# Batch 0's shuffle split between SBUF-to-SBUF moves and DRAM, and later shuffles sent in two parts, in a fused DFT and gated-MLP kernel

## The chip, the cores and the metric

The kernel runs on one core of a Trainium2 chip. The metric is the device time of one execution in microseconds (us). Before the change nine runs gave a median of 633.46 us (630.8 to 638.19). One further execution was profiled; all durations of single instructions come from it.

The engines are TensorE (PE; its weight loads are shown apart as PEld), VectorE (DVE), ScalarE (ACT), GpSimd (POOL) and SyncE (SP, which here only issues transfers). Every engine works through its own queue in order. Transfers are issued by SP, ACT and POOL and carried out by the core's 16 DMA engines.

## The reference, cut to what matters

```python
x = 0.1 * randn(8, 3008, 256)                      # batch, sequence, width; f32
X = fft(fft(x, axis=1), axis=2).real               # along the sequence, then along the width
X = X.reshape(24064, 256)
out = (relu(X @ w_gate) * (X @ w_val)) @ w_out     # 256 -> 1536 -> 256, f32
```

## The kernel before, in words

**Sequence DFT in two stages.** 3008 = 94 x 32. A batch lies in SBUF with 94 partitions and 32 rows j of 256 numbers in each. Since x is real, row j and row 32 - j are folded into one another (`fold`, on POOL, for batches 1 to 7), which leaves 17 rows in the tile `eo`. Stage 1 (`stage1`, line 152) multiplies each of 16 rows j by a table `w1[:, j, :]` of 96 columns: 48 frequencies, cosine and sine. The result goes through PSUM into the tile `t1` (96 partitions, 16 rows j). Stage 2 contracts over j and over cosine and sine, so these must become partitions: `t4` has 128 partitions (4 groups of frequencies x cosine or sine x 16 rows j) and 12 blocks of 256 numbers. The way from t1 to t4 is the **shuffle**: `shuffle_out` (line 202) writes t1 to a DRAM buffer `Td`, and `shuffle_in` (line 207) reads it back in the other order, in pieces of 512 bytes. `rotate` (line 213) then mends one column of t4 by a small matmul with the matrix `rot` and a copy back, and `stage2` (line 221) multiplies by the table `m2` and leaves `pq`, the operand of the MLP. Its second half (cs = 1) also sends one row to DRAM and back as a broadcast, `nb`.

**The width DFT** is folded into the weights: `pair_w` adds and subtracts the halves of a weight, `fold_w` (line 281) multiplies by cosines and sines of the width, and `wc`, `ws` and `wm` are the weights that the MLP uses.

**Start.** Batch 0 isn't folded. Its rows come by six loads on POOL's queue (`load_first`, line 119) that cast f32 to bf16: rows 0 to 15 into the tile `lo` by plain loads, rows 16 to 31 in mirrored order into `hi` by indirect loads. Each partition gets four or eight rows as one contiguous piece. `first_products` (line 180) then does stage 1 with separate matmuls for both tiles, in the groups of pairs c = (1, 2, 3), (4, 5) and (6, 7, 0), where pair c holds the rows 2c and 2c + 1; `evacuate` (line 167) copies each pair from PSUM to t1 on ACT or DVE. Batch 0's t1 leaves in four transfers (pairs 1 to 3, 4 and 5, 6 and 7 on SP; pair 0 on ACT), and comes back in two on SP (blocks 0 to 3, then 4 to 11), ahead of the loads of the other weights. `warm` (line 348) issues matmuls on a tile of zeros (`wk`, into `psk`): 11 at the start, 10 after the products, 7 more (line 490) ahead of the first rotate. Only blocks 0 to 3 are rotated before the main loop; the others at its step 4 (line 683).

**Main loop.** 288 steps of 8 batches x 3 blocks x 12 slices of the MLP's inner width. A step t does the gate's and the value's matmuls for one slice (lines 557, 558, 564 and 572), and the output matmuls of the block before (line 621). Work on the next batch is put between the steps by hand: `at(t, ...)` lists what is issued at a step, `plan` gives the steps of the eight stage 1 pairs of the next batch, `sh`, `tr` and `t2` those of its shuffle, rotate and stage 2. `pace` hands the steps of `fold` to POOL at a fixed rate. A later batch's shuffle leaves in one transfer (768 KB) after the eighth pair and comes back in one.

Of the kernel before, what the change touches and what calls it, by code (L numbers as in the profile page):

```python
# [43 lines left out]
def kernel(ctx: ExitStack, tc, x, w_gate, w_val, w_out, out):  # L44
# [32 lines left out]
    JH, PAD = NB // 4, 4  # L77
# [18 lines left out]
    def fold(b, eng):  # L96


        eo = xt[b]["eo"] = tp.tile([96, J, D], BF16, tag="eo", name="eo")[0:NA]
        for half, chunks in enumerate(((1, 3, 5, 7), (9, 11, 13))):  # L100
            for lo in chunks:
                xl, xh = xt[b][half]
                n, o = (3 if lo == 13 else 2), lo - half * (JH + 1)
                x1, e1, m = xl[0:NA, o:o + n, :], eo[:, lo:lo + n, :], (NB // 2 - lo - (0 if half else JH)) * D
                eng.tensor_tensor(free(e1, 0, [D, n], [H, 2]), free(x1, 0, [D + PAD, n], [H, 2]),
                                  free(xh[0:NA], m, [-D, n], [H, 2]), op=ALU.add)
                yield eng.tensor_tensor(x1[:, :, 1:D], x1[:, :, 1:D],  # L107
                                        free(xh[0:NA], m + D - 1, [-D, n], [-1, D - 1]), op=ALU.add)
                for op, o in ((ALU.add, 1), (ALU.subtract, H + 1)):
                    yield eng.tensor_tensor(e1[:, :, o:o + H - 1], x1[:, :, 1:H],  # L110
                                            free(x1, D - 1, [D + PAD, n], [-1, H - 1]), op=op)
            src, j = xt[b][half][0][0:NA, JH - 1 if half else 0, :], J - 1 if half else 0
            eng.tensor_copy(free(eo[:], j * D, [H, 2]), free(src, 0, [H, 2]))
# [5 lines left out]
    def load_first(r, n):  # L119

        name = "lo" if r < NB // 2 else "hi"
        if name not in xt.setdefault(0, {}):
            xt[0][name] = tp.tile([96, J, D], BF16, tag="eo", name=name)
        dst = xt[0][name][:, r % 16:r % 16 + n, :]
        if r < NB // 2:
            nc.gpsimd.dma_start(out=dst, in_=view(x, r * D, [[NB * D, 96], [1, n * D]]))
        else:
            k = {(24, 8): 0, (20, 4): 1, (16, 4): 2}[r, n]
            nc.gpsimd.indirect_dma_start(
                out=dst.rearrange("p j d -> p (j d)"), out_offset=None,  # L130
                in_=view(x, 0, [[n * D, NB // n * NA], [1, n * D]]),
# [20 lines left out]
    def stage1(b, c, evac):  # L152

        ps, eo = borrow("ps1"), xt[b]["eo"]
        for i in range(2):
            jj = 2 * c + i
            o = ps[0:96, i * D:(i + 1) * D]
            if jj:
                nc.tensor.matmul(o, lhsT=w1[:, jj, :], rhs=eo[:, jj, :], start=True, stop=True)  # L159
                continue  # L160
# [19 lines left out]
    def first_products(c, upper):  # L180
# [3 lines left out]
        for i in range(2):  # L184
            jj = 2 * c + i
            o = psf[c][0:96, i * D:(i + 1) * D]
            v = xt[0]["hi"][0:NA, 0 if jj == 0 else NB // 2 - jj, :] if upper else xt[0]["lo"][0:NA, jj, :]
# [19 lines left out]
    def shuffle_in(b, a0, a1):  # L207
        if b not in t4t:
            t4t[b] = tp.tile([128, NKA, D], BF16, tag="t4", name="t4")
        nc.sync.dma_start(out=t4t[b][:, a0:a1, :],  # L210
                          in_=view(Td[b], a0 * 128 * D, [[D, 128], [128 * D, a1 - a0], [1, D]]))

    def rotate(b, a0=0, a1=NKA, evac=nc.scalar.copy):
        t4 = t4t[b]
        ps = borrow("psr") if b or a0 else early("psr")
        nc.tensor.matmul(ps[:, a0:a1], lhsT=rot[:], rhs=t4[:, a0:a1, H], start=True, stop=True)
        evac(t4[:, a0:a1, H], ps[:, a0:a1])
# [85 lines left out]
    with tc.tile_pool(name="sp", bufs=1, space=SB) as sp:  # L303
# [24 lines left out]
        ki = sp.tile([NA, NKA, 4], F32, tag="ki")  # L328
# [8 lines left out]
        di = sp.tile([128, 4, 2, 16], F32, tag="di")  # L337
        ro = sp.tile([128, 4, 2, 16], F32, tag="ro")
# [17 lines left out]
        iota(pl, ki[:], [[1, NKA], [NKA, 4]], 0, 0)  # L356
# [18 lines left out]
        iota(pl, di[:], [[-32, 4], [-16, 2], [-1, 16]], 0, 1)  # L375
# [10 lines left out]
        def table(a, b_):  # L386
            cosines(free(w1[:], 96 * a, [96, b_ - a], [2, 48]), tq[:, a:b_, :], S)
            sines(free(w1[:], 96 * a + 1, [96, b_ - a], [2, 48]), tt[:, a:b_, :], S, -1.0)
# [28 lines left out]
        jj, sl, up = bits(0, 15), bits(4, 1), bits(5, 3)  # L417
# [5 lines left out]
        both = (free(tt[:], 0, [16 * 48, 2], [1, 48]), free(tq[:], 0, [16 * 48, 2], [1, 48]))  # L423
        cosines(free(wz[:], 0, [97, 2], [2, 48]), both[1], S)
        for k in range(2):
            sines(free(wz[:], 192 * (k + 1), [97, 2], [2, 48]), both[0], S, 2.0 * k - 1.0)
# [33 lines left out]
        evacuate(0, 7, psf[7], "dve")  # L460
        evacuate(0, 0, psf[0], "act")
        shuffle_out(0, 6, 8)
        shuffle_out(0, 0, 1, nc.scalar)
# [4 lines left out]
        shuffle_in(0, 0, 4)  # L468
        shuffle_in(0, 4, NKA)
# [3 lines left out]
        pl.tensor_scalar(ro[:, :, 0, 1:16], di[:, :, 0, 1:16], scalar1=16.0, scalar2=-1.0,  # L473
                         op0=ALU.is_equal, op1=ALU.mult)
        pl.tensor_scalar(ro[:, :, 1, 1:16], di[:, :, 1, 1:16], scalar1=-16.0, scalar2=None, op0=ALU.is_equal)
        pl.tensor_scalar(ro[:, :, :, 0], di[:, :, :, 0], scalar1=0.0, scalar2=None, op0=ALU.is_equal)
        pl.tensor_copy(rot[:], ro[:].rearrange("p u s j -> p (u s j)"))
        pl.iota(ix[:], pattern=[[-1, 2], [4 * NA, B]], base=4 * NA - 1, channel_multiplier=-4)
        pl.tensor_scalar(ix[:], ix[:], scalar1=0, scalar2=None, op0=ALU.max)

# [8 lines left out]
        psk = psg.tile([128, 512], F32, tag="g", name="psk")  # L489
        warm(7)  # L490
        rotate(0, 0, 4, dve.tensor_copy)
# [15 lines left out]
        for k in range(3, 12):  # L507
# [175 lines left out]
    at(4, rotate, 0, 4, NKA)  # L683
# [9 lines left out]
    for b in range(B - 1):  # L693
# [4 lines left out]
        at(t0 + sh, shuffle_out, b + 1, 0, 8)  # L698
        at(t0 + sh, shuffle_in, b + 1, 0, NKA)
        at(t0 + tr, rotate, b + 1)  # L700
        for i, k in enumerate(t2):
            at(t0 + k, stage2, b + 1, i // 2, i % 2, "act")
# [7 lines left out]
    def pace(t):  # L710

        paced["due"] += 0 if t < 12 else 1 if t < 23 else 0.75 if t < 54 else 23 / 36
# [83 lines left out]
```

## Time and profile before

| | |
|---|---|
| median of nine runs | 633.46 us (630.8 to 638.19) |
| profiled execution, its own time | 636.28 us |
| span of the profiled execution, first to last instruction | 634.1 us |
| TensorE busy | 620.2 us, 98% |
| VectorE busy | 536.1 us, 85% |
| ScalarE busy | 438.9 us, 69% |
| GpSimd busy | 517.7 us, 82% |
| DMA | 69.03 MB, mean 109 GB/s |
| mean granted TensorE clock | 0.989 |

In the lines of the profile, L592 is line 592 of the kernel before, `a<-b` says that a was written from b, and xN counts instructions. A line of waits names the engine, line and tile that waited, what released it, and then the total in us, how often, and the longest. A piece of the chain has its start and its duration in us. The granted clock is a share of TensorE's full speed; a table by stage gives it for each stretch of time.

### The profile page before, as it was taken

The numbers are of one execution on the slowest core, as the hardware profiler recorded it, in microseconds if no ns is written. First come the engines' busy times: TensorE is split into PE (matmuls) and PEld (weight loads), VectorE is DVE, ScalarE is ACT, GpSimd is POOL, SyncE is SP. The second block draws the span as 40 slices with busy tenths as digits, with TensorE's granted clock in tenths as the row PEclk, the third lists the DMA queues.
The fourth block names the chain that finished last, engine by engine and source line by source line (L and its number), as shares of the span: only waits on it lengthen the run. The fifth ranks groups of instructions, "written<-read, shape, count | busy, mean of one in ns | idle before, by whom it ended". The sixth has DMA issues, their size and how long they took to land.

```text
span 634.1 us, 12016 instructions
## 1 busy us (share of the span) xinstructions
PE 620.2 (98%) x4322; PEld 415.8 (66%) x4322; DVE 536.1 (85%) x641; ACT 438.9 (69%) x842; POOL 517.7 (82%) x443
## 2 busy tenths in 40 slices
PE   8999998999999999999999999999999999999996
PEld 6524665666667666666666666666666666666665
DVE  5567886899988988898988989889988999899991
ACT  4357776777777777777687777776777777766661
POOL 7089898999988999888988999889888966555665
PEclk7799999999999999999999999999999999999999
DMA  8579427442726146531836137342643123312114
GB/s 184 191 160 171 101 83 190 113 109 76 206 69 143 39 131 168 126 93 36 226 85 149 34 91 206 93 107 62 188 89 79 34 82 100 73 36 63 36 34 98
DMA packets 44050, 69.03 MB, mean 109 GB/s; under 512 B 5969, under 2 KB 33498, under 8 KB 41974
## 3 DMA queue, kind: packets, MB, share of 16 engines
q1 hardware_dynamic: 39062, 52.08, 32.5%
q0 software_dynamic: 4656, 15.88, 10.6%
q8 instruction: 34, 0.56, 0.4%
q10 hardware_dynamic: 272, 0.30, 0.2%
q14 instruction: 26, 0.21, 0.1%
HBM read 39.63 MB, written 30.96 MB: 111 GB/s over the span
## 4 chain that ended last, share of the span: by engine, by line
PE 95%; DMA 2%; DVE 1%; issue 0%; POOL 0%; ACT 0%; POOLq 0%; ACTq 0%; DVEq 0%
PE po L621 39%; PE V L572 19%; PE G L564 10%; PE G L557 9%; PE G L558 9%; PE psw L285 2%; PE ps L159 2%; PE ps L197 2%; PE ps L228 2%; DMA hi<-in_x_dram,ixf 1%; DMA t<-Td 1%; PE psk L351 1%; DMA Td<-t 1%; DVE h L585 0%; PE ps L163 0%
## 5 line engine op out<-in xcount | busy, mean ns | idle before, releaser
L592 POOL TENSOR_TENSOR h<-gm,E 128x992 bf16<-128x992 f32 (+1 forms) x138 | 319.8, 2318 | 80.1 <-DVE E L599 48.1
L621 PE MATMUL po<-wo,h 128*128 128x256 bf16 (+2 forms) x2304 | 328.6, 272 | 0.0
L621 PEld LDWEIGHTS <-h 128*128 128x128 bf16 (+2 forms) x2304 | 231.3, 103 | 105.9
L566 ACT ACTIVATE gm<-G 128x496 f32<-128x496 f32 (+1 forms) x288 | 170.5, 592 | 93.9 <-PE G L564 86.3
L585 DVE TENSOR_TENSOR h<-gs,V 128x1024 bf16<-128x1024 f32 (+3 forms) x150 | 173.8, 1159 | 62.8 <-PE V L572 47.8
L579 DVE SCALAR_TENSOR_TENSOR E<-nb,af,V 128x496 f32<-128x496 bf16 (+1 forms) x276 | 190.2, 731 | 0.0
L559 ACT ACTIVATE gs<-G 128x497 f32<-128x497 f32 (+2 forms) x288 | 169.6, 589 | 25.0 <-PE G L558 25.0
L599 DVE SCALAR_TENSOR_TENSOR E<-E,V 128x992 f32<-128x992 f32 (+1 forms) x138 | 164.4, 1192 | 0.0
L564 PE MATMUL G<-pq,wm 128*128 128x496 bf16 (+1 forms) x288 | 108.0, 375 | 0.3 <-ACT gs L559 0.2
L557 PE MATMUL G<-pq,wc 128*128 128x497 bf16 (+2 forms) x288 | 107.9, 375 | 0.0
L558 PE MATMUL G<-pq,ws 128*128 128x497 bf16 (+2 forms) x288 | 107.9, 375 | 0.0
L572 PE MATMUL V<-pq,ws 128*128 128x497 bf16 (+2 forms) x288 | 85.4, 374 | 0.0
L572 PE MATMUL V<-pq,wc 128*128 128x497 bf16 (+2 forms) x288 | 85.4, 375 | 0.0
L558 PEld LDWEIGHTS <-ws 128*128 128x128 bf16 x288 | 28.2, 98 | 32.6
L634 ACT COPY os<-po 128x512 f32<-128x512 f32 x63 | 36.9, 586 | 14.4 <-PE po L621 13.5
L174 ACT CAST t<-ps 96x512 bf16<-96x512 f32 x60 | 35.0, 583 | 12.4 <-PE ps L197 10.0
L572 PEld LDWEIGHTS <-wc 128*128 128x128 bf16 x288 | 28.2, 98 | 21.1 <-issue 3.0
L110 POOL TENSOR_TENSOR eo<-xla 94x254 bf16<-94x254 f32 x56 | 40.3, 727 | 0.7
L557 PEld LDWEIGHTS <-wc 128*128 128x128 bf16 x288 | 28.2, 98 | 18.5 <-issue 1.3
L107 POOL TENSOR_TENSOR xla<-xla,xha 94x510 f32<-94x510 f32 x28 | 35.5, 1267 | 2.2
L110 POOL TENSOR_TENSOR eo<-xlb 94x254 bf16<-94x254 f32 (+1 forms) x42 | 34.1, 815 | 0.6
L564 PEld LDWEIGHTS <-wm 128*128 128x128 bf16 x288 | 28.1, 98 | 7.5 <-issue 4.9
(119 smaller groups left out, 377.2 us busy)
## 6 DMA issues: line engine op xcount, KB each, us to landing
out_dram<-os SPq DMA_DIRECT2D x124, 128.0 KB
Td<-t SPq DMA_DIRECT2D x7, 768.0 KB
t<-Td SPq DMA_DIRECT2D x7, 768.0 KB
out_dram<-os SPq DMA_DIRECT2D x82, 64.0 KB
xla<-in_x_dram SPq DMA_DIRECT2D x7, 720.0 KB
xlb<-in_x_dram SPq DMA_DIRECT2D x6, 640.0 KB
nb<-Nd SPq DMA_DIRECT2D x23, 128.0 KB
out_dram<-os SPq DMA_DIRECT2D x40, 48.0 KB
```

What stands on the lines that cost most here:

```text
L110: yield eng.tensor_tensor(e1[:, :, o:o + H - 1], x1[:, :, 1:H], free(x1, D - 1, [D + PAD, n], [-1, H - 1]), op=op)
L557: nc.tensor.matmul(G[:, ds], lhsT=wc[0][:, fs], rhs=pq[:, 0, ds], start=True, stop=False)
L558: nc.tensor.matmul(G[:, ds], lhsT=ws[0][:, fs], rhs=pq[:, 1, ds], start=False, stop=True)
L559: nc.scalar.activation(pair(t, "gs")[:, t % 2, ds], G[:, ds], ACTF.Relu)
L564: nc.tensor.matmul(G[:, cols], lhsT=wm[0][:, f * 128:(f + 1) * 128], rhs=pqt[b, blk][:, 1, cols], start=False, stop=True, skip_group_check ...
L566: nc.scalar.activation(pair(t, "gm")[:, t % 2, cols], G[:, cols], ACTF.Relu)
L572: nc.tensor.matmul(pair(t, "V")[:, t % 2, cs], lhsT=w[:, f * 128:(f + 1) * 128], rhs=pqt[b, blk][:, min(k, 1), cs], start=(k == 0), stop=( ...
L579: nc.vector.scalar_tensor_tensor(pair(t, "E")[:, t % 2, cols], nbt[b, blk][:, cols], af[:, f:f + 1], pair(t, "V")[:, t % 2, cols], op0=ALU ...
L585: nc.vector.tensor_tensor(pair(t, "h")[:, k, 0, 0:ds.stop - ds.start], pair(t, "gs")[:, k, ds], pair(t, "V")[:, k, ds], op=ALU.mult)
L592: eng.tensor_tensor(free(pair(t, "h")[:], 1024 * (t % 2) + 512 + w - 1, [1024, n], [-1, w]), pair(t, "gm")[:, k, cols], val[:, k, cols], o ...
L599: nc.vector.scalar_tensor_tensor(E[:, :, cols], E[:, :, cols], 2.0, V[:, :, cols], op0=ALU.mult, op1=ALU.subtract)
L621: nc.tensor.matmul(po[0:m, i, :], lhsT=pair(t - f + ff, "h")[:, ff % 2, sg, g * 128:g * 128 + m], rhs=wo[:, ff, :], start=(ff == 0), stop= ...
```

## The change

- Batch 0's rows j = 0, 1 and 12 to 15 no longer pass through DRAM: for each, one transfer (`spread`) goes from t1 (96 partitions x 512 bytes) to t4 (8 partitions x 12 blocks). Three are issued by SP, three by ACT. Rows 2 to 11 go through Td as before, in two writes by SP, and come back by one read that POOL issues.
- For this the order of t4's partitions changes from (group, cosine or sine, j) to (j, group, cosine or sine). The columns of w1 and wz, the matrix rot and the index bits behind m2 change with it.
- Batch 0's t4 is rotated once, all 12 blocks, before the main loop. The seven `warm` matmuls ahead of it are gone, and so is the rotate at step 4.
- Later shuffles leave in three transfers: pairs 1 to 5 one step after the fifth pair's stage 1, then pairs 6 and 7, then pair 0. The read waits for all three and is in the new order.
- The loads of batch 0's rows ask for rows of 256 numbers (512 bytes in bf16): `lo` has rows at a distance of 258 numbers, and the source of `hi` is given row by row. The tile of `eo` has the same padded rows.
- stage2 does cs = 1 ahead of cs = 0 in the main loop, for batches 1 to 7. One step of batch 1's fold moves from before the main loop into it.

```diff
-    JH, PAD = NB // 4, 4
+    JH, PAD, DP = NB // 4, 4, D + 2
...
-        eo = xt[b]["eo"] = tp.tile([96, J, D], BF16, tag="eo", name="eo")[0:NA]
+        eo = xt[b]["eo"] = tp.tile([96, J, DP], BF16, tag="eo", name="eo")[0:NA]
...
-            xt[0][name] = tp.tile([96, J, D], BF16, tag="eo", name=name)
-        dst = xt[0][name][:, r % 16:r % 16 + n, :]
+            xt[0][name] = tp.tile([96, J, DP], BF16, tag="eo", name=name)
+        dst = xt[0][name][:, r:r + n, 0:D] if r < NB // 2 else free(xt[0][name][:], r % 16 * D, [1, n * D])
         if r < NB // 2:
-            nc.gpsimd.dma_start(out=dst, in_=view(x, r * D, [[NB * D, 96], [1, n * D]]))
+            nc.gpsimd.dma_start(out=dst, in_=view(x, r * D, [[NB * D, 96], [D, n], [1, D]]))
         else:
...
-                out=dst.rearrange("p j d -> p (j d)"), out_offset=None,
-                in_=view(x, 0, [[n * D, NB // n * NA], [1, n * D]]),
+                out=dst, out_offset=None,
+                in_=view(x, 0, [[n * D, NB // n * NA], [D, n], [1, D]]),
...
-    def shuffle_in(b, a0, a1):
+    def t4_of(b):
         if b not in t4t:
             t4t[b] = tp.tile([128, NKA, D], BF16, tag="t4", name="t4")
-        nc.sync.dma_start(out=t4t[b][:, a0:a1, :],
-                          in_=view(Td[b], a0 * 128 * D, [[D, 128], [128 * D, a1 - a0], [1, D]]))
+        return t4t[b]
+
+    def shuffle_in(b, j0, j1, q=nc.sync):
+        q.dma_start(out=t4_of(b)[8 * j0:8 * j1, :, :],
+                          in_=view(Td[b], j0 * D, [[D, j1 - j0], [16 * NKA * D, 8], [16 * D, NKA], [1, D]]))
+
+    def spread(jj, q):
+        q.dma_start(out=t4_of(0)[8 * jj:8 * jj + 8, :, :], in_=t1t[0][:, jj, :])
...
         evacuate(0, 6, psf[6], "act")
         evacuate(0, 7, psf[7], "dve")
+        spread(12, nc.scalar)
         evacuate(0, 0, psf[0], "act")
-        shuffle_out(0, 6, 8)
-        shuffle_out(0, 0, 1, nc.scalar)
+        spread(13, nc.sync)
+        spread(14, nc.sync)
+        spread(15, nc.sync)
+        spread(0, nc.scalar)
+        spread(1, nc.scalar)
...
-        shuffle_in(0, 0, 4)
-        shuffle_in(0, 4, NKA)
         load_w(1, nc.sync)
         load_w(2, nc.sync)
...
         pl.tensor_scalar(ix[:], ix[:], scalar1=0, scalar2=None, op0=ALU.max)
+        shuffle_in(0, 2, 12, pl)
...
-        psk = psg.tile([128, 512], F32, tag="g", name="psk")
-        warm(7)
-        rotate(0, 0, 4, dve.tensor_copy)
+        rotate(0, dve.tensor_copy)
         stage2(0, 0, 0, "act")
...
-        for k in range(3, 12):
+        for k in range(3, 11):
             next(first)
...
-    at(4, rotate, 0, 4, NKA)
...
-        at(t0 + sh, shuffle_out, b + 1, 0, 8)
-        at(t0 + sh, shuffle_in, b + 1, 0, NKA)
+        at(t0 + plan[min(b, 1)][4] + 1, shuffle_out, b + 1, 1, 6)
+        at(t0 + sh, shuffle_out, b + 1, 6, 8)
+        at(t0 + sh, shuffle_out, b + 1, 0, 1)
+        at(t0 + sh, shuffle_in, b + 1, 0, 16)
         at(t0 + tr, rotate, b + 1)
         for i, k in enumerate(t2):
-            at(t0 + k, stage2, b + 1, i // 2, i % 2, "act")
+            at(t0 + k, stage2, b + 1, i // 2, 1 - i % 2, "act")
...
-        paced["due"] += 0 if t < 12 else 1 if t < 23 else 0.75 if t < 54 else 23 / 36
+        paced["due"] += 0 if t < 12 else 1 if t < 24 else 0.75 if t < 54 else 23 / 36
```

## The prediction

> **What bounds the kernel now.** I read the page first, then who waited for whom on TensorE, then a table by stage, then the chain in two stretches, then the transfers.
>
> The page (engine, busy us, share of the span, instructions):
>
> ```profile
> span 634.1 us, 12016 instructions
> PE 620.2 (98%) x4322; PEld 415.8 (66%) x4322; DVE 536.1 (85%) x641; ACT 438.9 (69%) x842; POOL 517.7 (82%) x443
> PE 95%; DMA 2%; DVE 1%; issue 0%; POOL 0%; ACT 0%; POOLq 0%; ACTq 0%; DVEq 0%
> ```
>
> TensorE is busy for 98% and carries 95% of the chain. Only two things shorten the run: fewer matmuls, or one of its few waits gone. These are the waits (total us, times, longest):
>
> ```profile
> PE psr L216 <- DMA t<-Td: 2.6, 1, 2.6
> PE V L572 <- DVE h L585: 1.5, 2, 1.0
> PE ps L197 <- DMA hi<-in_x_dram,ixf: 1.4, 1, 1.4
> PE psk L351 <- DVE wk L345: 1.3, 1, 1.3
> PE psw L285 <- ACT t L217: 0.5, 1, 0.5
> PE ps L197 <- DMA lo<-in_x_dram: 0.3, 1, 0.3
> ```
>
> The change touches the first, the third, the fifth and the sixth. The table by stage (us; busy of PE, PEld, DVE, ACT, POOL; granted clock; DMA share; GB/s):
>
> ```profile
> 0.00:9.00 9.00, 6.08 (x35) 3.02 (x36) 5.88 (x21) 5.46 (x11) 7.12 (x21) 0.99 0.72 113
> 9.00:20.50 11.50, 11.36 (x105) 11.24 (x105) 5.27 (x17) 2.77 (x8) 4.52 (x15) 0.50 0.65 184
> 20.50:24.00 3.50, 3.50 (x12) 1.25 (x12) 3.40 (x9) 1.25 (x3) 0.00 (x0) 0.71 0.29 84
> 24.00:29.50 5.50, 5.44 (x32) 1.94 (x28) 1.99 (x5) 1.75 (x3) 0.00 (x0) 1.00 0.94 299
> ```
>
> The products of batch 0 (line 197) run 9.14 to 20.44 at clock 0.50, although TensorE is never idle there. POOL is idle from 20.5 to 29.5. The chain around batch 0's shuffle and around batch 1's (start us, us, what):
>
> ```profile
> 20.44 3.24 PE psk L351 x10
> 23.68 2.73 PE psw L285 x12
> 26.41 1.62 PE psk L351 x7
> 28.02 0.05 PE psr L216
> 28.10 0.19 DVE t L217
> ...
> 89.16 0.59 ACT t L174
> 89.75 0.02 issue
> 89.77 4.28 DMA Td<-t
> 94.05 0.02 issue
> 94.06 5.34 DMA t<-Td
> ```
>
> In the first stretch the 17 matmuls on zeros (psk) cover the shuffle; the seven at 26.41 are themselves on the chain. In the second nothing covers the trip out and back: TensorE came to the rotate at 96.82 and started it at 99.45.
>
> **The change part by part.**
>
> *Seven warming matmuls go.* Line 490 took 1.62 us. The rotate can start at 26.41 if all twelve blocks of t4 are in SBUF; before, it needed only four. DVE, which copies its result, is busy until 26.74 (wm, 26.39 + 0.35) and did that copy at 28.10 before; so the pair rotate and copy comes 1.45 us earlier, not 1.62. The gates follow the same steps behind it. Gain 1.45 us; ends 0 (t4 lands at 28) and 1.62.
>
> *When t4 is complete.* Rows 2 to 11: their last part leaves after c=5 is evacuated (15.34 + 0.69); in the transfers from 17.0 to 20.5 the engines fall idle at 17.8, so I take 18.2 for its completion, and POOL then issues one read. An issue of 128 pieces cost 0.60 (two weights, 1.19), one of 1536 pieces 1.10 (wo): by interpolation 960 cost 0.9. From POOL's first issue (lo, 1.40) to the first busy slice of the engines (2.75) pass 1.35 us, so data flow from about 19.6; 1536 pieces of 512 bytes took 95.1 to 98.9, 3.7 us, in t<-Td, so 960 take 2.3, twice that if spread badly: landed at 22.4 to 24.7. The six direct moves: number 12 leaves after c=6 (19.34), 13 to 15 on SP after c=7 (20.31), 0 and 1 on ACT after c=0 (21.06). ACT's issue of Td took 0.35, so the last starts at 21.44. The equal issue of 96 rows at 21.09 let SP go on at 23.05, 1.96 us later; the last move lands at 23.4, and up to 1.5 later as weight loads now share the engines. All before 26.4: the margin is 1.5 to 3 us, and I put the wait at nothing. What is under that cover: psk and psw on TensorE, 20.44 to 26.41.
>
> The Trainium skill, "DMA: Bandwidth & Descriptors", on why a DMA increments its semaphore by 16, speaks against this part: a transfer uses the largest number of engines up to 16 that divides both slowest dimensions, which makes 8 of a move from 96 partitions to 8, and 10 of the read into 80. By it each move puts 12 pieces on an engine and all six put 72 on the same eight; I estimate 1 us more, still before 26.4, and the sum is the same.
>
> *Behind the added waits.* POOL now waits for Td in front of the weight pairs (line 497). They started at 31.51, after POOL had waited 17.63 us for the weights; the wait to 18.2 and the 0.9 us issue lie inside. ACT issues three moves in place of one Td: sin (line 467) comes 0.35 later, 21.83; DVE's second pair then ends near 24.4 for a product at 25.5. Covered. SP no longer waits at 23.05 for Td: the eight weight loads (24.03 on) start near 21, so POOL's pairs and folds start up to 3 us earlier; nothing on TensorE waited for these.
>
> *The second rotate goes.* At step 4 TensorE waited 0.45 us for ACT's copy of the last eight blocks (41.95). Gain 0.45; ends 0.2 and 0.65 with the matmul and copy.
>
> *Rows in 512-byte pieces.* Rows of batch 0 came in 4 KB (later 2 KB) pieces, cast from f32. The nearest row is wo: same queue, same cast, 1536 pieces of 512 bytes, 195 GB/s from 53.3 to 57.4; lo and hi together had 162 GB/s from 2.8 to 8.9. The same 0.79 MB would take 4.0 us in place of 6.1, less a ramp that wo's window leaves out; and issues grow by (1.10 - 0.60) / 1408 x 672 = 0.24 us. No row has an indirect issue in pieces. Lower bound: its excess over a direct one (1.18 - 0.67 = 0.51 for 96 rows), charged per piece, is 5.3 ns, 4.1 us for 768, so hi 3.6 us later. Upper bound: all of 1.41 + 0.34 gone. I take wo's side with about 0.9 us of ramp and start: 0.6 us gained on the wait of 1.41. Later rows have room: the products at half clock take 11.3 us, and 0.79 MB at 195 GB/s takes 4.
>
> *Later shuffles in two parts.* Five of eight pairs leave earlier, and only three after c=7 and c=0. At 89.77 the remaining piece is 96 rows of 1 KB, like ACT's Td of batch 0: 1.96 us in place of 4.28. The read starts 2.32 earlier and the stall shrinks from 2.64 to 0.3. The read's new order (t4's rows by j) has no row: if it runs as the old, 5.34; a third more for the pieces (3.7 becomes 4.9) leaves a gain of 1.1; upper end 2.64. I take 2.3. Batches 2 to 7 never waited: the next read began at 160.05, with 5.34 it lands at 165.4, and the rotate came at 168.46; 3.1 us of slack grow by 2.3. Two more SP issues of 0.31 a batch lie there too, and the first part's output goes ahead of row stores that nobody waits for.
>
> *At nothing:* column order of w1, wz, rot (same instruction counts; sines 0.60 and cosines 0.73 end before the rows land), padded rows of eo, stage2's sine half first. One fold step moves behind the loop's start: POOL sat idle 2.99 us at 63.3; without that cover a stage1 product at step 24 would wait up to 0.9 us.
>
> **Sum.** 0.6 + 1.45 + 0.45 + 2.3 = 4.8 us. The profiled execution took 636.28 (span 634.1, 2.2 around it); it would take 631.5. It stands 2.8 above the median of nine, 633.46, so the median goes to 628.7.
>
> **Rivals.**
>
> *A: slower; t4 late and the clock falls.* The seven matmuls also kept TensorE busy. The idle 7.73 to 9.14 (1.41 us) was followed by clock 0.50 for 13.6 us (by stretches of one us: 0.93 in 8 to 9, 0.50 from 9 to 22, 0.75 in 22 to 23). If t4 lands after 27.8, TensorE is idle as long; at half clock it loses up to 6.8 us of the next 13.6, the gain of 1.45 is gone, and 0.6 + 0.45 + 2.3 - 6.8 is 3.4 us slower: 636.9. For it: the new paths have no row. Against: 1.5 us of margin. It decides from 27.8 on.
>
> On this the Trainium skill's "TensorE: Matmul & The Clock Gate", Part 1, differs from the row: there an idle window of about 3.4 us is needed for the fall, and a busy one lifts the clock. The trace shows a fall after 1.41 us, and 11.3 busy us that did not lift it. By the page A would cost the idle alone, and the time would be near 630.
>
> *B: rows later.* The indirect issue pays by the piece: 0.6 becomes -3.6, the sum 0.6, the time 632.9; half of that, 630.8. For it: 1.18 us for only 96 rows. Against: wo's 1.10 for 1536.
>
> *C: the second shuffle is slower or its stall moves.* 1.1 in place of 2.3 and rows at 0: sum 3.0, 630.5.
>
> *D: rows so early that the clock holds.* If the idle before 9.14 nearly closes and the clock stays, the 11.3 us of line 197 halve: some 5 more, 623.7. Against: 11 busy us of these products left the clock at 0.50.
>
> **How the numbers follow.** Forecast 0.62 (628.7, alone 626.5 to 631), A 0.10, B 0.12, C 0.11, D 0.05. 0.5% is 3.2 us, about what can be told from no change: the border is 630.3, and 636.6 above. Faster: nearly all of the forecast with D and a little of C: 0.67. Same: B, C and the forecast's rest: 0.24. Slower: most of A: 0.09. The range leaves D and most of A out and takes in B's end of 632.9 and the scatter of a median of runs that span 630.8 to 638.2: 625.2 to 634.2.
>
> **What would show it.** Right: rotate within 0.2 us of the last psw, no wait on t<-t or t<-Td before it; no wait of psw on the rotate's copy; the wait at the second rotate under 0.8 us; hi's wait under 1 us. Wrong: psr waiting for a transfer at 26 to 30 with a clock under 1.00 behind it (A); POOL's indirect issue over 2 us (B); t<-Td over 6 us (C); line 197 at 0.05 us a matmul (D).

## The result, and the profile after

The changed kernel takes 641.31 us (median of 10 executions, 638.27 to 642.65), against 633.71 us for the kernel before, run beside it (31 executions). The ratio is 1.0108 [1.0081, 1.0135]: slower by 6.8 us of 634. The forecast was 628.7 us, 0.8% faster; rival A, the one that ended slower, had the mechanism.

The profiled execution took 640.17 us (span 638.4), 3.9 above that of before, while the medians are 7.6 apart: the profiled execution of before stood above its median and this one below. The page of the changed kernel (engine, busy us, share of the span, instructions; then the chain by engine):

```profile
span 638.4 us, 12033 instructions
PE 621.4 (97%) x4314; PEld 415.9 (65%) x4314; DVE 538.1 (84%) x641; ACT 438.9 (69%) x841; POOL 520.6 (82%) x444
...
PE 93%; DMA 4%; DVE 1%; POOL 0%; issue 0%; ACT 0%; POOLq 0%; DVEq 0%; SPq 0%
```

TensorE has eight matmuls fewer (seven on zeros, one rotate) and yet 1.2 us more busy time, which points to a lower clock; the share of DMA on the chain went from 2 to 4%. The waits of TensorE (total us, times, longest):

```profile
PE psr L222 <- DMA wst<-in_moe_w_val_dram: 3.6, 1, 3.6
PE V L581 <- DVE h L594: 2.3, 3, 1.4
PE ps L197 <- DMA hi<-in_x_dram,ixf: 1.9, 1, 1.9
PE psk L357 <- DVE wk L351: 1.3, 1, 1.3
PE psr L222 <- DMA t<-Td: 1.1, 1, 1.1
PE ps L197 <- ACT w L319: 0.6, 1, 0.6
```

The first line is the new one: the rotate of batch 0 (psr) stood for 3.6 us. The releaser named, a weight load, is the last event that the profile could match; the rotate reads only t4 and rot, and experiment 1 shows the same instruction waiting for `t<-t`, the direct moves. By the semaphores of the trace the last of the six moves landed at 30.93, 0.13 us ahead of the rotate; POOL's read of the other rows had landed at 27.55. The wait for hi grew from 1.41 to 1.95 us (1.9 here). The wait at batch 1's rotate (`t<-Td`) shrank from 2.64 to 1.07, and psw no longer waits for ACT's copy after the second rotate. By stage (us; busy of PE, PEld, DVE, ACT, POOL; granted clock; DMA share; GB/s):

```profile
0.00:9.00 9.00, 6.39 (x35) 3.11 (x36) 5.86 (x21) 5.16 (x11) 7.01 (x17) 1.00 0.70 96
9.00:20.50 11.50, 10.25 (x97) 10.25 (x97) 4.89 (x15) 2.74 (x7) 6.58 (x20) 0.53 0.79 197
20.50:24.00 3.50, 3.50 (x18) 1.87 (x17) 2.65 (x6) 0.64 (x2) 0.85 (x1) 0.61 0.36 90
24.00:27.40 3.40, 3.40 (x15) 0.94 (x13) 2.64 (x6) 1.22 (x3) 0.00 (x0) 1.00 0.90 195
27.40:31.00 3.60, 0.02 (x1) 0.00 (x0) 0.28 (x1) 0.59 (x1) 0.00 (x0) 0.87 0.76 239
31.00:37.30 6.30, 6.03 (x20) 2.00 (x21) 3.44 (x5) 2.52 (x5) 4.91 (x4) 0.53 1.02 270
```

Between 27.4 and 31.0 TensorE does nothing, and the six busy us behind it run at clock 0.53. Most of the loss is here. Along the chain (start us, us, what):

```profile
20.48 7.56 DMA t<-t
...
28.06 2.97 DMA wst<-in_moe_w_val_dram
...
31.06 0.18 PE psr L222
```

```profile
95.50 1.79 DMA Td<-t
...
97.34 6.22 DMA t<-Td
...
103.61 0.19 PE psr L222
```

The rotate of batch 0 starts 3.0 us later than before (31.06 against 28.02). Where TensorE next waits for h behind the start of the main loop, 64.02 against 58.31, it is 5.7 behind. Batch 1's shuffle gives 1.5 back (103.61 against 99.45, 4.2 behind): its last write takes 1.79 in place of 4.28, its read 6.22 in place of 5.34. The end is 4.3 behind.

### The profile page after: what moved, and what is told of

Its sections match the earlier page's. It is cut to its first block, busy times and chain, and to the rows that moved or that the text cites. A ratio compares the mean times of both kernels' runs of the same rounds, so it can differ in the third digit from the quotient of the medians.

```text
span 638.4 us, 12033 instructions
## 1 busy us (share of the span) xinstructions
PE 621.4 (97%) x4314; PEld 415.9 (65%) x4314; DVE 538.1 (84%) x641; ACT 438.9 (69%) x841; POOL 520.6 (82%) x444
## 4 chain that ended last, share of the span: by engine, by line
PE 93%; DMA 4%; DVE 1%; POOL 0%; issue 0%; ACT 0%; POOLq 0%; DVEq 0%; SPq 0%
PE po L630 39%; PE V L581 19%; PE G L566 9%; PE G L573 9%; PE G L567 9%; PE ps L159 2%; PE ps L234 2%; PE ps L197 2%; PE psw L291 1%; DMA t<-t 1%; DMA hi<-in_x_dram,ixf 1%; DMA t<-Td 1%; DVE h L594 1%; DMA wst<-in_moe_w_val_dram 0%; DMA Td<-t 0%
## 5 line engine op out<-in xcount | busy, mean ns | idle before, releaser
L643 ACT COPY os<-po 128x512 f32<-128x512 f32 x63 | 36.9, 586 | 14.3 <-PE po L630 11.7
L581 PEld LDWEIGHTS <-wc 128*128 128x128 bf16 x288 | 28.2, 98 | 22.4 <-issue 4.3
```

Of the source, the lines that this page charges most:

```text
L581: nc.tensor.matmul(pair(t, "V")[:, t % 2, cs], lhsT=w[:, f * 128:(f + 1) * 128], rhs=pqt[b, blk][:, min(k, 1), cs], start=(k == 0), stop=( ...
```

## The experiments

The ratios are to the kernel before, run beside each on the same chip. "Changed kernel" and "before" name the two kernels of this case.

**1. Seventeen matmuls on zeros in the idle time ahead of the rotate.**

```diff
 # changed kernel
+        psk = psg.tile([128, 512], F32, tag="g", name="psk")
+        warm(17)
         rotate(0, dve.tensor_copy)
```

> The changed kernel with 17 matmuls on zeros put between the last psw and the rotate, some 3.7 us at full clock, as long as the rotate waited. Theory 1 (the idle of 3.64 us let the clock fall, and the half clock after it costs more than the wait): the rotate still starts near 31, the clock stays 1.00 from 24 on, no stretch at 0.50 after 30, and the run is 2.5 to 5 us shorter than the changed kernel, 636 to 639 us. Rival (the wait alone is the loss; the clock costs little): within 1 us of the changed kernel's 641.3.

Measured: 640.62 us, ratio 1.0063 [1.0026, 1.0101]. The wait, now short and rightly named, and the stretches behind it:

```profile
PE psr L222 <- DMA t<-t: 0.4, 1, 0.4
```

```profile
30.00:31.60 1.60, 1.18 (x6) 0.36 (x5) 0.00 (x0) 0.00 (x0) 0.00 (x0) 1.00 1.07 357
31.60:37.30 5.70, 3.68 (x20) 1.28 (x21) 3.99 (x7) 2.79 (x5) 4.43 (x4) 1.00 0.94 258
```

The clock stays at 1.00, the same 20 matmuls take 3.68 us where they took 6.03, and the rotate still starts at 31.60. So the clock's fall behind the idle time is real, and t4 is late all the same. By these matmuls the clock alone is worth 2.4 us. The ratio fell by 0.0045, 2.9 us, with intervals that overlap; by the medians alone the gain is 0.7 us, as the rival had it, but the kernel before, run beside it, was 1.2 us higher too. So the clock is some 2 to 3 us of the 6.8, and the times by themselves don't show even that.

**2. Batch 0's rows loaded in long pieces again, all else changed.** The pieces of 512 bytes come off both loads, and the rows of `lo` lie without the padding again.

```diff
-            nc.gpsimd.dma_start(out=dst, in_=view(x, r * D, [[NB * D, 96], [D, n], [1, D]]))
+            nc.gpsimd.dma_start(out=dst, in_=view(x, r * D, [[NB * D, 96], [1, n * D]]))
...
-                in_=view(x, 0, [[n * D, NB // n * NA], [D, n], [1, D]]),
+                in_=view(x, 0, [[n * D, NB // n * NA], [1, n * D]]),
```

> The changed kernel with batch 0's rows loaded as before: contiguous pieces of eight and four rows. Theory (the small pieces cost issue time on POOL and bring nothing): POOL's first issue is back at 0.67 us, the wait for hi ends near 9.2 instead of 10.25, all that follows is 1.1 us earlier, and the rotate starts near 30; 640 us. Rival (the rows are not what delays the start, the moves set the rotate): the rotate stays near 31 and the time at 641.

Measured: 642.15 us, ratio 1.0105 [1.0038, 1.0173]. In the profiled execution the products ran at full clock and were done near 14.5, six us early. POOL's issue of the read, the rotate, and the stages:

```profile
19.41 1.21 POOL L213 DMA_DIRECT2D t<-Td  x1 [4.88 <-DMA Td<-t]
...
31.40 0.18 PE L222 MATMUL psr<-t,rot 128*128 128x12 bf16 x1 [9.56 <-DMA t<-Td]
```

```profile
22.00:31.40 9.40, 0.00 (x0) 0.10 (x1) 0.00 (x0) 0.47 (x1) 3.77 (x4) 0.72 1.06 238
31.40:36.40 5.00, 5.00 (x18) 1.67 (x18) 2.23 (x3) 1.76 (x3) 4.79 (x4) 0.50 1.00 214
```

The rotate did not move: the rival had that right, and the theory's 30 and 640 us were missed. The moves did follow the products: the last of them landed at 22.51, against 30.93 in the changed kernel. POOL's read did not. Td's second write took 4.76 us (13.94 to 18.7), the read 11.95 from its issue (it landed at 31.36), and the DMA engines are full (share 1.06) with weights that SP was free to load early. So t4 as a whole doesn't follow the products: with slow products the moves land last, with fast ones the read does.

**3. SP's weight loads held until t4 is there.** A transfer of two numbers per partition from t4 to DRAM waits for all moves and the read, and the four pairs of weight loads of two slices stand behind it on SP.

```diff
-        load_w(1, nc.sync)
-        load_w(2, nc.sync)
+        late = lambda: (load_w(1, nc.sync), load_w(2, nc.sync))
...
         shuffle_in(0, 2, 12, pl)
+        nc.sync.dma_start(out=Sd, in_=t4t[0][:, 0, 0:2])
+        late()
```

> The changed kernel with the weight loads of parts 1 and 2 held back on SP by a small transfer that reads t4, so that they start only when all of t4 has landed. Theory a (the direct moves sit on few DMA engines and share them with the loads and POOL's read): the moves end 1.5 to 3 us earlier, the rotate starts at 28 to 29.5, and the wait of 3.64 us falls to 1 to 2. Theory b (the moves are slow by themselves, in issue and in their pieces, whatever else is under way): the rotate stays at 30.5 to 31.1.

Measured: 646.47 us, ratio 1.0157 [1.0089, 1.0225]; the rotate starts at 29.08, two us sooner, and a later wait takes over:

```profile
PE V L583 <- DVE h L596: 11.1, 2, 10.6
...
PE psr L223 <- DMA t<-t: 1.4, 1, 1.4
```

Without the weight loads beside them the moves landed at 28.9 and the rotate came two us sooner, as theory a had it. So weight loads sharing the DMA engines account for two of the late microseconds and the rest belongs to the moves and POOL's read, which still run beside one another; and the loads cannot be put behind t4, because the main loop needs them.

**4. Only the later shuffles in parts.** The old order of t4, and everything else as before.

```diff
 # before
-        at(t0 + sh, shuffle_out, b + 1, 0, 8)
+        at(t0 + plan[min(b, 1)][4] + 1, shuffle_out, b + 1, 1, 6)
+        at(t0 + sh, shuffle_out, b + 1, 6, 8)
+        at(t0 + sh, shuffle_out, b + 1, 0, 1)
```

> The kernel before with one part of the change alone: later shuffles leave in three transfers (pairs 1 to 5, then 6 and 7, then 0), the read in its old order. Theory (this part is a gain of its own; what remained of the wait in the changed kernel, 1.07 us, is the new read order): the wait of the rotate of batch 1 falls from 2.64 to 0.2 to 0.5 us and the run is 2.2 us shorter, 631.5 us. Rival (the wait only moves: the write of the first part delays the row stores or the time between 60 and 90 us): wait gone, but time within 0.8 us of before.

Measured: 632.12 us (628.77 to 636.83), ratio 0.9946 [0.9909, 0.9984]: 3.4 us faster by the ratio, 2.8 by the medians. The longest and the shortest of TensorE's waits of half a microsecond or more:

```profile
PE V L572 <- DVE h L585: 2.8, 3, 1.9
PE ps L197 <- DMA hi<-in_x_dram,ixf: 1.7, 1, 1.7
...
PE V L572 <- DVE E L579: 0.5, 1, 0.5
PE psw L285 <- ACT t L217: 0.5, 1, 0.5
```

The wait of psr for t<-Td (2.6 before) is gone from the list. This part does what was forecast.

**5. The changed kernel without direct moves.** All rows go through Td; SP reads all sixteen in the new order, ahead of the weight loads.

```diff
-        spread(12, nc.scalar)
         evacuate(0, 0, psf[0], "act")
-        spread(13, nc.sync)
-        spread(14, nc.sync)
-        spread(15, nc.sync)
-        spread(0, nc.scalar)
-        spread(1, nc.scalar)
+        shuffle_out(0, 6, 8)
+        shuffle_out(0, 0, 1, nc.scalar)
+        shuffle_in(0, 0, 16)
         load_w(1, nc.sync)
...
-        shuffle_in(0, 2, 12, pl)
```

> The changed kernel with only the direct moves undone: all rows of batch 0 go through DRAM as before (pairs 6 and 7 on SP, pair 0 on ACT), and SP reads all twelve blocks at once, ahead of the weight loads, in the new order. Theory 1 (the path of moves and POOL's read, with the weight loads let in front, is what makes t4 late and independent of how fast the products run): the read starts about 2 us after the last evacuation and takes 5.5 to 6.5 us, the rotate starts at 29 to 30.5 in an execution with slow products and near 24 to 25 in one with fast products, and the median is 3 to 5 us under the changed kernel, 636 to 638. Rival (the rotate of twelve blocks at once and the missing seven matmuls are the loss, the path does not matter): within 1.5 us of 641.

Measured: 638.89 us, ratio 1.0048 [1.0019, 1.0078], 3.8 us less than the changed kernel. The moves with POOL's read lose that. Even without them the rotate waits, for a read of 6.29 us (rotate at 30.68, clock 0.50 from 29.6 to 36.4):

```profile
22.41 1.85 DMA Td<-t
...
24.35 6.29 DMA t<-Td
```

Against the profile of the changed kernel, whose products ran at half clock too, the rotate is only 0.4 us earlier. The executions' times show the rest: four of experiment 5, with a mean clock of 0.992 or more, took 634.9 to 636.1 us, the eight others 638.8 to 641.4; the changed kernel's one at 0.992 took 640.0, and experiment 2, whose profiled products ran at full clock, stayed at 640.6 to 643.9. Without the moves and POOL's read the kernel gains from early products; with them it does not.

**6. The read of rows 2 to 11 on SP, ahead of its three moves, in place of POOL.**

```diff
         shuffle_out(0, 4, 6)
+        shuffle_in(0, 2, 12)
...
-        shuffle_in(0, 2, 12, pl)
```

> The changed kernel with the read of rows 2 to 11 issued by SP, right behind the write that it waits for and ahead of the moves and the weight loads, instead of by POOL. Theory a (DMA engines 0 to 7 are shared by the read and the moves, one after the other makes 5 to 6 us from 22 to 28): the read is done by 23 to 24, the moves end near 27, the rotate starts at 28 to 28.5, and the time is 2 to 4 us under the changed kernel, 637 to 639. Theory b (the moves alone are the last to land, by their issue): rotate still at 30 to 31, time 640 to 641.

Measured: 639.3 us, ratio 1.007 [1.0041, 1.0099], 2.4 us less than the changed kernel (the intervals overlap). The rotate is at 31.04, and what it waits for are the moves:

```profile
PE psr L222 <- DMA t<-t: 2.6, 1, 2.6
```

The read landed at 27.28, hardly sooner than from POOL (27.55), and the last move at 30.79. So with slow products the moves land last whichever queue the read is on; they ran beside the read and the first weight loads here too, so this isn't their price alone.

**7. Experiment 4 without the seven matmuls on zeros ahead of the first rotate.**

```diff
-        psk = psg.tile([128, 512], F32, tag="g", name="psk")
-        warm(7)
         rotate(0, 0, 4, dve.tensor_copy)
```

> The kernel before with later shuffles in three transfers (as e4) and without the seven matmuls on zeros ahead of the first rotate, which still takes only four blocks. Theory (the prediction's term: the first blocks are there by then, the seven matmuls were on the path): the rotate starts with a wait under 0.5 us, 1.2 to 1.5 us earlier than in e4, and the time is 1.2 us under e4's, 631. Rival (the seven matmuls covered the read and held the clock): the rotate waits 1 us or more for the read, the clock falls in some executions, time equal to or up to 2 us over e4's 632.1.

Measured: 631.95 us, ratio 0.9945 [0.9916, 0.9974], the same as experiment 4. No gain from leaving out the seven matmuls shows, though the times, known to some 3 us, don't rule out the 1.45 of the forecast. In the profiled execution the rotate, now free of them, waits for the read of four blocks,

```profile
PE psr L216 <- DMA t<-Td: 1.7, 1, 1.7
```

as the rival had it, and experiment 4, with them, waits 2.8 us in all for h later on. The two profiles took different courses (products at full clock here, at half clock in experiment 4), so that the 1.45 is waited for at the next arrival is likely, not shown.

**8. Experiment 4 with batch 0's rows as in the changed kernel** (rows of 256 numbers asked for, rows at a distance of 258 in `lo`, the padded tile).

```diff
-    JH, PAD = NB // 4, 4
+    JH, PAD, DP = NB // 4, 4, D + 2
...
+            nc.gpsimd.dma_start(out=dst, in_=view(x, r * D, [[NB * D, 96], [D, n], [1, D]]))
...
+                in_=view(x, 0, [[n * D, NB // n * NA], [D, n], [1, D]]),
```

> The kernel before with later shuffles in three transfers (as e4) and batch 0's rows loaded in rows of 256 as in the changed kernel. Theory (the row form costs POOL 0.4 us at its first issue and 0.2 at the index instruction, and the later start lets the clock fall more often): hi's wait ends near 10.2 in place of 9.1 to 9.5, the clock of the products is 0.50 in most executions, and the time is 1 to 4 us over e4's, 633 to 636. Rival (the rows are nothing): 632.

Measured: 635.04 us, ratio 1.0002 [0.9972, 1.0033]: 0.0056, or 3.6 us, above experiment 4, as the theory had it. The row loads on POOL's queue in the changed kernel, and the product that waits for hi:

```profile
1.45 1.10 POOL L126 DMA_DIRECT2D lo<-in_x_dram  x1 [0.32 <-issue]
3.77 1.04 POOL L129 DMA_INDIRECT hi<-in_x_dram,ixf  x1 [0.29 <-POOL ixf L366]
...
10.25 0.37 PE L197 MATMUL ps<-hi,w 94*96 94x129 bf16 x2 [1.95 <-DMA hi<-in_x_dram,ixf]
```

Before, these stood at 1.40 (0.67 long), 3.05 (1.18) and 9.14. The plain issue is 0.43 longer and the index computation behind it 0.23, so hi's issue starts 0.72 later and the products 1.1. In experiment 8 itself the plain issue took 0.95, hi's began 0.35 later than before and the products 0.98 (10.12): the rest of the delay lies in the transfers. In the packets of the trace only `lo` came in pieces of 512 bytes; `hi` stayed in pieces of 4 and 2 KB. The 768 pieces of the first `lo` took 3.16 us from first to last, the 96 long ones before 3.08: nothing gained there. The mean clock was 0.990 or less in 11 of 12 executions, against 5 of 12 in experiment 4.

**9. The hole filled: experiment 4 with seven matmuls on zeros between the first and the second group of products**, where TensorE waits for hi.

```diff
+        warm(7)
         jj, sl, up = bits(0, 15), bits(4, 1), bits(5, 3)
```

> The kernel before with the later shuffles in parts, and seven matmuls on zeros between the first group of products and the second, where TensorE waited 1.4 us for hi. Theory (the hole lets the clock fall, and whether it comes back in the products makes most of the scatter from run to run): the wait before the second group is under 0.5 us, the clock stays at 1.00 from 6 us through the products, which end near 15 to 16 instead of 20.4, the mean clock is 0.995 or more in nearly every run, and the time is 629 to 630, 2 to 3 less than with the later shuffles in parts alone (632.1). Rival (products of this kind don't hold the clock, hole or no hole): the clock is 0.50 from about 10 on all the same, the mean clock scatters as before, and the time is 632 with 0.5 either way.

Measured: 630.09 us (628.84 to 632.3), ratio 0.9941 [0.9907, 0.9974]. Two of the stages:

```profile
9.00:15.00 6.00, 6.00 (x105) 5.84 (x104) 4.82 (x16) 2.74 (x7) 4.52 (x15) 1.00 1.03 263
15.00:22.00 7.00, 6.76 (x29) 2.88 (x28) 5.01 (x12) 2.44 (x5) 0.00 (x0) 1.00 0.55 184
```

The products run at clock 1.00 and end near 15 in place of 20.4; the clock was 0.994 or more in every execution (experiment 4: 7 of 12), and none was above 632.3. The theory of the clock holds. The time is 2 us under experiment 4's median, but the kernel before, run beside it, was lower too, and by the ratios the two are not told apart. This version beats both kernels of the case, as do experiments 4 and 7.

**10. The same fill, nine matmuls, in the changed kernel.**

```diff
+        warm(9)
         jj, sl, up = bits(3, 15), bits(0, 1), bits(1, 3)
```

> The changed kernel with nine matmuls on zeros between the first group of products and the second. Theory (t4 is late by its transfers, which do not start much earlier when the products end earlier, since the reads and moves end behind weight loads and each other): the products may run at full clock, but the first rotate still starts at 29 to 31, behind a wait of 4 to 10 us, the clock is 0.50 for some us behind it, and the time is 638.5 to 641. Rival (t4 follows the products, and late products make the whole loss): the rotate starts at 24 to 27, and the time is 634 to 636.

Measured: 642.5 us, ratio 1.0129 [1.0073, 1.0185]. The products are at full clock, and then:

```profile
23.00:32.20 9.20, 0.02 (x1) 0.04 (x1) 0.00 (x0) 0.58 (x1) 3.53 (x3) 0.76 1.01 227
32.20:38.00 5.80, 5.79 (x20) 1.98 (x20) 3.00 (x7) 2.27 (x4) 3.16 (x3) 0.50 1.08 187
```

TensorE stands for 9.2 us before the rotate at 32.21. The same five us that help the kernel before do nothing here: the end is set by t4, as in experiment 2, even later than the theory's 29 to 31 and 638.5 to 641. The moves had landed at 22.27, POOL's read, issued at 21.06, at 32.16.

**11. Experiment 7 with one read of all twelve blocks, in the old order, and one rotate.**

```diff
-        shuffle_in(0, 0, 4)
-        shuffle_in(0, 4, NKA)
+        shuffle_in(0, 0, NKA)
...
-        rotate(0, 0, 4, dve.tensor_copy)
+        rotate(0, 0, NKA, dve.tensor_copy)
...
-    at(4, rotate, 0, 4, NKA)
```

> The kernel before with the later shuffles in parts, one read of all twelve blocks of batch 0's t4 in the old order, one rotate of all twelve, and no matmuls on zeros ahead of it. Theory (waiting for twelve blocks in place of four is itself a loss, whatever the way): the rotate waits 2 to 4 us for the read, the clock is 0.50 for some us behind it, and the time is 634 to 636, 2 to 4 more than with two rotates and no matmuls on zeros (632.0). Rival (the new order of the read and of t4 makes the loss of 3.8 us that the changed kernel without moves showed over the small rows alone): the wait is under 2 us and the time is 631 to 632.5.

Measured: 633.66 us (631.63 to 638.31), ratio 1.0007 [0.9971, 1.0042], 3.9 us above experiment 7. The rotate waited only 0.8 us; TensorE then waited 3.0 us for h and lost the clock there (0.50 from 33.7 to 40.5). The wait was smaller than the theory said, the loss as large: it gave away what parting the later shuffles had won. In the profile the wait for h stands behind VectorE's two adds of a weight pair:

```profile
30.36 1.75 DVE L277 TENSOR_TENSOR wst<-wst 128x512 f32<-128x512 f32 x1
...
32.15 1.63 DVE L279 TENSOR_TENSOR wst<-wst 128x512 f32<-128x512 f32 x1
```

In the kernel before and in experiment 7 each of them took 0.68 to 0.69. In experiment 4, whose products ran at half clock as here, the first took 0.68, the second 1.64, and the wait for h was 1.9. Here both ran beside GpSimd's adds of another pair, which began at 30.27, since the rotate started 0.7 us later (27.53 against 26.8): the 1.1 more of the wait is the first add. That one rotate of twelve blocks costs 3.9 is shown by the times; by which way is read from one execution each and stays open.

**12. The new order of t4 on top of that**, with rows in long pieces: the changed kernel of experiment 5 with the edit of experiment 2.

> The changed kernel without direct moves, its rows 2 to 11 and the six others through DRAM and one read on SP, and with batch 0's rows loaded in long pieces as before. It differs from the kernel with one read and one rotate in the old order (633.7) by the new order of t4, with what follows from it. Theory (the new order's read is slower, 6.3 us in the run without moves against 4.7 in the old order, and the rows are a loss of their own of about 2.9): batch 0's read takes 6 us or more, the rotate waits 2 us or more for it, and the time is 635 to 637, with the runs without moves (638.9) 2 to 4 above. Rival (the order costs nothing here; the 6.3 was of the short row pieces and what came late behind them): the read takes 4.5 to 5, the wait is under 1.2 us, and the time is 633 to 634.

Measured: 635.6 us, ratio 1.0035 [0.9999, 1.0071]. Batch 0's read in the old order (experiment 11) and in the new (this one):

```profile
22.75 4.74 DMA t<-Td
```

```profile
18.84 6.65 DMA t<-Td
...
25.53 0.18 PE psr L222
```

The read in the new order takes 1.9 us more, and the rotate waited 4.70 for it; batch 1's read, with no weight loads beside it, took 6.17 here and 5.22 in experiment 11. The read in the new order is slower in itself, as the theory had it. Experiment 12 also differs from 11 by the other small parts of the change (padded rows of eo, the order of stage 2's halves, one moved step of the fold), which no run tests by themselves.

**The ladder.** Steps are differences of ratios times 634 us:

| kernel | ratio to before | step, us |
|---|---|---|
| later shuffles in parts (4) | 0.9946 [0.9909, 0.9984] | -3.4 |
| seven matmuls gone (7) | 0.9945 [0.9916, 0.9974] | -0.1 |
| one read, one rotate (11) | 1.0007 [0.9971, 1.0042] | +3.9 |
| new order of t4, with the small parts (12) | 1.0035 [0.9999, 1.0071] | +1.8 |
| rows in 512-byte pieces (5) | 1.0048 [1.0019, 1.0078] | +0.8 |
| direct moves and POOL's read (changed kernel) | 1.0108 [1.0081, 1.0135] | +3.8 |

They add up to the 6.8 measured. With half-intervals of 0.003 to 0.004 on both sides a single step is known to some 2.4 to 3.2 us: the first, third and last are shown, the 1.8 rests on the traces besides, and the rows cost 3.6 alone (8 against 4, known to 3.1) and little where t4 is late anyway (0.8; experiment 2 against the changed kernel, 0.2). The steps also hold chance: which course the clock takes in the products differs from execution to execution (below), and experiment 7 had 2 of 12 executions under a mean clock of 0.990, experiments 4 and 11 had 5.

## Why the prediction was wrong

Against the forecast of -4.8 us the ladder gives +6.8, 11.6 apart: later shuffles 1.1 better than put (-3.4 for -2.3), seven matmuls 1.35 worse, one read and rotate 4.35 worse (+3.9 for -0.45), the order of t4 1.8, the rows 1.4 (+0.8 for -0.6), the moves and POOL's read 3.8, the last and the order having been put at nothing on batch 0's path. Each of these differences is known to some 3 us only.

*"When t4 is complete", put at 23.4 with no wait, is the step that failed.* TensorE was ready at 27.42, the last move landed at 30.93 and the rotate started at 31.06. The issues of the read and of the moves:

```profile
20.15 1.20 POOL L213 DMA_DIRECT2D t<-Td  x1 [4.77 <-DMA Td<-t]
...
20.48 2.36 SPq L217 DMA_DIRECT2D t<-t  x3
20.48 1.30 ACTq L217 DMA_DIRECT2D t<-t  x1
...
22.43 1.47 ACTq L217 DMA_DIRECT2D t<-t  x2
```

Its terms, forecast and measured:

| term | forecast | measured |
|---|---|---|
| Td's second write complete | 18.2 | 19.45 |
| from there to POOL's issue of the read | none | 0.70 (20.15) |
| POOL's issue of the read | 0.9 | 1.20 |
| the read landed | 22.4 to 24.7 | 27.55 |
| issue of one move | 0.35 | 0.66 to 1.30 |
| last move issued | 21.44 | 23.9 |
| from there to its landing | 1.96, up to 1.5 more | 7.0 (30.93; last piece at 30.0) |

The issues came late in part because the rows were (1.1 us); the large miss is the transfers' own duration. The row that I took for a move, 96 rows of 1 KB in 1.96 us, was of a time when the DMA engines were nearly idle (share 0.29), and the 1.5 us that the prediction allowed for sharing with the weight loads was too little. In 24.0 to 27.4, where the moves ran, the share is 0.90: by the packets of the trace about 0.35 of it are the first two of SP's eight weight loads (issued from 22.88), 0.23 POOL's read and 0.33 the moves. SP issued the six other loads from 28.06 on only.

What this company costs can be read from the same six moves, from the end of the last issue to the last landing: 2.8 us in experiment 10 and 4.2 in experiment 2, where they ran ahead of POOL's read; 4.7 in experiment 3, beside the read but without the loads; 7.0 in the changed kernel, beside both. So 1.96 with 1.5 more was right for moves with little beside them (2.8), and wrong for the moves as the change sends them. Where the moves were early, the read came last: 11.1 us (experiment 10) and 11.95 (experiment 2) from its issue, beside all the weight loads, where the prediction's terms give 4.2 to 6.5 (from 18.2 to 22.4 or 24.7).

Before, the read stood ahead of the loads on one queue. With fast products that order tells: a read of 768 KB ahead of the loads took 6.65 us (experiment 12), POOL's of 480 KB beside them 11.95 (experiment 2). With slow products it does not (experiment 6). How much of this is the order and how much the other queue, no run parts.

On the number of engines the Trainium skill, "DMA: Bandwidth & Descriptors" (why a DMA increments its semaphore by 16), agrees with the traces: the landing of each move is counted in eight steps (changed kernel), that of the read, where SP issues it, in ten (experiment 6). My estimate from it, 1 us more, was far too low for what came: even with the weight loads held back the moves landed at 28.9 (experiment 3). What eight engines in place of 16 cost by themselves, no run shows.

*Rival A was right in mechanism and had its price split wrongly.* It asked for t4 after 27.8, an idle as long as 1.41 us, and then clock 0.50. All of that came (0.50 from 30.1 to 36.9, 6.83 us). I charged the fall 6.8 and the idle time nothing but the lost 1.45. A stretch of 6.83 at half clock can lose at most 3.4, and experiment 1 puts it at 2 to 3; the late start of everything behind the rotate (3.0 in the profile) is the larger part. The chance of 0.10 rested on "1.5 us of margin", and every term of that margin was an estimate from a row under other conditions.

*"Seven warming matmuls go", 1.45:* no gain shows (0.1 in experiment 7, known to some 3), and its rotate waited 1.7 for the read. I named what would be late next only up to 27.8 and took the margin of four blocks for one of twelve.

*"The second rotate goes", 0.45:* the wait went as forecast, but its condition, one rotate of all twelve blocks, costs 3.9 (experiment 11). Two rotates let stage 2 start on a third of the data; the sum priced the instruction and not the dependence, nor what the later start brings together on VectorE and GpSimd.

*"Rows in 512-byte pieces", 0.6 gained, lost 3.6 alone.* The issue's growth, put at 0.24, was 0.43 and moved the index computation behind it as well (with it 0.72 of the 1.1 us, the rest is in hi's transfer); the transfer's gain, taken from `wo`, did not come, and `hi` was not cut at all. Rival B had the sign and the size (-3.6) with another cause: not the indirect issue, which took 1.04 where it took 1.18 before, but the plain one ahead of it and the transfers.

*"Later shuffles in two parts", 2.3,* was right: 2.8 to 3.4 alone. In the changed kernel the wait shrank by 1.57, since the new order's read takes 0.9 longer; the forecast had that as its lower side.

*Rival D was dismissed by a wrong reading.* I wrote that 11 busy us of these products left the clock at 0.50. They do not lift it once it has fallen; but they hold it if it has not (experiments 2, 7, 9, 10 and 12). And five us saved in the products bring two at the end at most, because the weights come next (a weight load of 4.73 us stands at 20.68 in the chain of experiment 9).

*The base.* One profiled execution was carried to the median by a constant 2.8. Executions of the kernel before fall by their clock: those of mean clock 0.992 or more average 633.3 us, the others 638.2 (64 and 32 executions). The products at half clock that I read in its table are one of two courses that it takes.

## What to carry to other kernels

A transfer's duration is only good for the company it was measured in: when a change takes a wait off a queue, list what that queue will issue next, and charge it to the transfers that run at that time. A read that stands ahead of bulk loads on their own queue has a lead that it can lose when it moves to another queue (6.65 us against 11.95, experiments 12 and 2). Where part of the data is enough to start, merging two small steps into one moves the start to the last piece, so price the dependence before the instruction.

## What the runs showed of the hardware

**The clock is granted in windows, and their phase differs from execution to execution.** In all 14 profiled executions every stretch of one clock in the first 50 us is a multiple of 3.41 us (3.41, 6.83, 10.24, 13.65, up to 23.9), counted from the first record of the clock, which lies 4.0 to 7.3 us behind the start. The busy time of TensorE in the window around the wait for hi, at clock 1.00, and the clock of the next window, for seven of them:

| execution | window from, us | busy in 3.41 us | next window |
|---|---|---|---|
| changed kernel | 6.2 | 1.51 | 0.50 |
| experiment 4 | 7.6 | 1.67 | 0.50 |
| experiment 11 | 6.3 | 1.89 | 0.50 |
| before | 5.4 | 1.95 | 0.50 |
| experiment 7 | 6.5 | 2.14 | 1.00 |
| experiment 2 | 5.7 | 2.23 | 1.00 |
| experiment 12 | 7.3 | 2.54 | 1.00 |

In the first 50 us of all of them no window with 2.0 us of work or more was followed by a fall; of those with 1.7 to 2.0 some were and some, with other matmuls in them, were not (1.91 in experiment 9). A wait of 1.4 us can thus cost nothing, or five us in the products, by where a window's edge falls in it. The Trainium skill, "TensorE: Matmul & The Clock Gate", Part 1, gives windows of about 3.4 us, which these stretches show; the window that it calls idle, though, need not be idle: 1.95 busy us of 3.41 were not enough.

Three windows filled with products (94 x 96, 129 columns; experiment 11, 9.8 to 20.0) did not raise the clock from 0.50. It rose behind the window in which the matmuls on zeros (128 x 128, 512 columns) began.

**A direct move from 96 partitions to 8 is slow to issue and late to start.** One issue took 0.66 to 1.33 us on SP or ACT in the six runs that have them, against 0.30 to 0.35 for a write to Td. The first piece moved 1.4 to 1.8 us after the issue began where no read of POOL's ran (experiments 2 and 10), and 2.5 to 3.2 where one did (changed kernel, experiments 1 and 3); with ACT's write to Td it was 0.85.

**An add on VectorE is slower beside one on GpSimd.** The add of a weight pair (128 x 512, f32) took 0.68 to 0.69 us alone, and 1.63 to 1.75 where it began while GpSimd's add of another pair ran (experiments 4, 5, 6, 8, 11 and 12).
